# Row sums first and inverted by VectorE, one out-projection burst per head pair, DMA transposes from batch 1 on: beacon attention with a gated feed-forward block

## The chip, the cores and the metric

The kernel runs on one core of one Trainium2 chip. The metric is the device time of one execution in microseconds (us), lower is better. "Span" is the time from the first to the last instruction in a profiled execution; where the record has both for one execution, the span is 1.7 to 2.1 us shorter than the time.

Engines are named as in the profile: PE is TensorE's matmuls, PEld its weight loads, DVE is VectorE, ACT is ScalarE, POOL is GpSimd, SP is the sync engine that issues DMAs. PSUM is the memory that these kernels' matmuls write to; they share it out in banks. In lines of the profile, x8 counts instructions, and a name such as s_ps is the tile written.

## The reference, cut to what matters

```python
B, H, S, Nb, D = (8, 8, 576, 16, 64)           # attention; D_MODEL = 512, D_FF = 1536
k_all = np.concatenate([beacon_k, k], axis=2)   # 16 beacon keys + 576 keys
v_all = np.concatenate([beacon_v, v], axis=2)
scores = 0.125 * np.matmul(q, k_all.transpose(0, 1, 3, 2))
scores = np.where(causal, -1e9, scores)         # beacons are always visible
a = np.exp(scores - max); a /= a.sum(-1)        # softmax
x = np.matmul(a, v_all) -> (4608 tokens, 512)
out = (gelu(x @ w_gate) * (x @ w_val)) @ w_out  # (4608, 512) float32
```

## The kernel before: the parts that matter

Everything is computed transposed: keys, or features, on partitions and tokens along the free dimension, in bf16. For each batch there is an attention stage (four pairs of heads) and then a gate/value stage for one chunk of 512 tokens (12 tiles, 96 matmuls of 512 columns). The out-projection of the chunk before (48 matmuls, called "O" below) is spread over the attention stage as filler. There are eight batches but nine chunks; the ninth is done in the tail.

For a pair, q and k arrive token by token and must be transposed before the scores. TensorE does that through a PSUM score buffer and DVE copies it out:

```python
def transpose_pair(b, m):                     # 11 TensorE transposes, 2 DVE copies
    t_ps = psum_s.tile([P, 2, 1024], BF16, tag="s")
    for w, src in enumerate((q_ring[...], k_ring[...])):
        for j in range(4): tr(t_ps[:, w, c], src[:, j, 2*m:2*m+2, :])
        ...
    keep(nc.vector.tensor_copy(qkT[:, :, NB:SK], t_ps[:, :, 0:576]))
    keep(nc.vector.tensor_copy(qkT[:, 1, 0:NB], t_ps[:, 1, 576:592]))
```

`scores(b, m, c)` computes one of four chunks of scores, which ACT turns into exps and POOL masks. `attend` multiplies each tile of exps by V (values) and by ones (row sums, the same sum on 64 partitions), both in one PSUM tile of three banks with a single buffer. `normalize` inverts the sums on ACT as exp(-ln z) and multiplies on DVE; only then is that tile free:

```python
act(ln_sb, x_ps[:, Z0 : Z0 + S], ACT.Ln)
act(rec_sb, ln_sb, ACT.Exp, scale=-1.0)
tensor_tensor(out=xT_sb[...], in0=x_ps[:, X0 : X0 + S], in1=rec_sb, op=mult)
```

The order per pair alternates small pieces:

```python
for m in range(1, NPAIR):
    scores(b, m, 0); scores(b, m, 1)
    av(m - 1, 0, 2);  o(4);  scores(b, m, 2)
    av(m - 1, 4, 1, 3)
    if m < NPAIR - 1: transpose_pair(b, m + 1)
    o(2);  normalize(b, m - 1);  scores(b, m, 3);  o(2)
```

The softmax here doesn't subtract the row's maximum and nothing guards it: scores larger than these inputs give would overflow.

Of the kernel before, what the change touches and what calls it, by code (L numbers as in the profile page):

```python
# [8 lines left out]
P = 128  # L9
# [7 lines left out]
CH = 512  # L17
N_CHUNKS = N_TOK // CH
NPAIR = H // 2
NPERM = 2  # L20
# [16 lines left out]

# [3 lines left out]
X0 = 16  # L41
Z0 = X0 + S
# [6 lines left out]
SET_EXP = "natural_log_exp_and_others"  # L49
# [4 lines left out]
def kernel(  # L54
# [21 lines left out]
    opool = ctx.enter_context(tc.tile_pool(name="opool", bufs=2))  # L76
# [3 lines left out]

    ident = const.tile([P, P], BF16, name="ident", tag="ident")
    ones = const.tile([P, D], BF16, name="ones", tag="ones")
    nc.vector.memset(ones, 1.0)
# [3 lines left out]
    xT_sb = const.tile([P, NPAIR, N_TOK], BF16, name="xT_sb", tag="xT_sb")  # L87

    NRING = 3
    q_ring, k_ring, v_ring, qk_ring = [], [], [], []  # L90
    for r in range(NRING):
        qt = ring.tile([P, 5, H, D], BF16, name=f"q_sb{r}", tag=f"q_sb{r}")
        kt = ring.tile([P, 5, H, D], BF16, name=f"k_sb{r}", tag=f"k_sb{r}")
        vt = ring.tile([P, 5, H, D], BF16, name=f"v_sb{r}", tag=f"v_sb{r}")
        q_ring.append(qt)
        k_ring.append(kt)
        v_ring.append(vt)
    for r in range(2):
        t = ring.tile([P, 2, 640], BF16, name=f"qkT{r}", tag=f"qkT{r}")
        nc.vector.memset(t[:, 1, SK:640], 0.0)  # L100
        qk_ring.append(t)

# [5 lines left out]

    def load_qk(b):
        for src, dst in ((q, q_ring[b % NRING]), (k, k_ring[b % NRING])):  # L110
            if b < NPERM:
                dma(
                    dst[:, 0:4, :, :].rearrange("p r h d -> p (r h d)").rearrange("p (h x) -> p h x", h=H),
                    src[b, :, 0:512, :].rearrange("h (p r) d -> p h (r d)", r=4),
                )
            else:
                for j in range(4):
                    dma(dst[:, j, :, :], src[b, :, j * P : (j + 1) * P, :].rearrange("h p d -> p h d"))
            dma(dst[0:64, 4, :, :], src[b, :, 512:576, :].rearrange("h p d -> p h d"))
        dma(k_ring[b % NRING][64:80, 4, :, :], beacon_k[b].rearrange("h t d -> t h d"))  # L120

    def load_v(b):
        dst = v_ring[b % NRING]
        dma(dst[0:NB, 0, :, :], beacon_v[b].rearrange("h t d -> t h d"))
        dma(dst[NB:P, 0, :, :], v[b, :, 0:112, :].rearrange("h p d -> p h d"))
        for j in range(1, 4):
            r0 = 112 + (j - 1) * P
            dma(dst[:, j, :, :], v[b, :, r0 : r0 + P, :].rearrange("h p d -> p h d"))
        dma(dst[0:80, 4, :, :], v[b, :, 496:576, :].rearrange("h p d -> p h d"))

    def load_gate_val(i):
        fs = slice(i * 512, (i + 1) * 512)
        for w, dst in ((moe_w_gate, wg_sb), (moe_w_val, wv_sb)):
            keep(nc.gpsimd.dma_start(out=dst[:, :, fs], in_=w[:, fs].rearrange("(kk p) f -> p kk f", p=P)))

    def load_out_w():
        keep(nc.gpsimd.dma_start(out=wo_sb, in_=moe_w_out.rearrange("(ii p) m -> p ii m", p=P)))
# [6 lines left out]


    def transpose_pair(b, m):
        i = b * NPAIR + m
        t_ps = psum_s.tile([P, 2, 1024], BF16, name="t_ps", tag="s")

        def tr(out_ap, in_ap, r0=0):  # L150
            n = in_ap.shape[0]
            keep(nc.tensor.transpose(out_ap, in_ap, ident[r0 : r0 + n, r0 : r0 + n]))  # L152

        for w, src in enumerate((q_ring[b % NRING], k_ring[b % NRING])):
            by_head = src[:, 0:4, :, :].rearrange("p r h d -> p (r h d)").rearrange(
                "p (h r d) -> p h r d", h=H, r=4
            )
            for j in range(4):
                c = slice(j * P, (j + 1) * P)
                if b < NPERM:  # L160
                    for hi in range(2):
                        tr(t_ps[64 * hi : 64 * hi + 64, w, c], by_head[:, 2 * m + hi, j, :])
                else:
                    tr(t_ps[:, w, c], src[:, j, 2 * m : 2 * m + 2, :])
            tr(t_ps[:, w, 512:576], src[0:64, 4, 2 * m : 2 * m + 2, :])
        tr(t_ps[:, 1, 576:592], k_ring[b % NRING][64:80, 4, 2 * m : 2 * m + 2, :], 64)
        qkT = qk_ring[i % 2]
        if b < NPERM:
            for w in range(2):
                keep(  # L170
                    nc.vector.tensor_copy(  # L171
                        qkT[:, w, NB : NB + 512].rearrange("p (t r) -> p t r", r=4),
                        t_ps[:, w, 0:512].rearrange("p (r t) -> p t r", r=4),
                    )
                )
            keep(nc.vector.tensor_copy(qkT[:, :, NB + 512 : SK], t_ps[:, :, 512:576]))
        else:
            keep(nc.vector.tensor_copy(qkT[:, :, NB:SK], t_ps[:, :, 0:576]))  # L178
        keep(nc.vector.tensor_copy(qkT[:, 1, 0:NB], t_ps[:, 1, 576:592]))  # L179

    exp_of = {}

    def scores(b, m, c):
        i = b * NPAIR + m
        qkT = qk_ring[i % 2]
        if c == 0:
            exp_of[i] = epool.tile([P, 2, EXP_W], BF16, name="expT", tag="expT")
        expT = exp_of[i]
        s_ps = psum_s.tile([P, 2, 512], FP32, name="s_ps", tag="s")
        for t, s_lo, w, col in CHUNKS[c]:  # L190
            for hi in range(2):
                r = slice(64 * hi, 64 * hi + 64)
                mm(
                    s_ps[:, hi, col : col + w],
                    qkT[r, 1, t * P : (t + 1) * P],
                    qkT[r, 0, NB + s_lo : NB + s_lo + w],
                    True,
                    True,
                )
        o, w = CHUNK_OFF[c], CHUNK_W[c]  # L200
        act(expT[:, :, o : o + w], s_ps[:, :, 0:w], ACT.Exp, scale=QK_SCALE)
        for t, s_lo, _, _ in CHUNKS[c]:
            if s_lo != S_LO[t]:
                continue
            d = expT[0 : KROWS[t], :, EXP_OFF[t] : EXP_OFF[t] + DIAG[t]]
            keep(
                nc.gpsimd.affine_select(  # L207
                    out=d,
                    in_=d,
                    pattern=[[0, 2], [1, DIAG[t]]],  # L210
                    compare_op=ALU.is_ge,
                    fill=0.0,
                    base=NB if t == 0 else 0,
                    channel_multiplier=-1,
                )
            )

    x_of = {}

    def attend(b, m, t):  # L220
        i = b * NPAIR + m
        if t == AV_ORDER[0]:
            x_of[i] = psum_x.tile([P, 1536], FP32, name="x_ps", tag="x")
        x_ps, expT, v_sb = x_of[i], exp_of[i], v_ring[b % NRING]
        kr, first, last = KROWS[t], t == AV_ORDER[0], t == AV_ORDER[-1]
        for base, split in ((X0, 496), (Z0, 432)):
            for q0, q1 in ((S_LO[t], split), (max(split, S_LO[t]), S)):
                if q0 >= q1:
                    continue
                e0 = EXP_OFF[t] + q0 - S_LO[t]  # L230
                for hi in range(2):
                    mm(
                        x_ps[64 * hi : 64 * hi + 64, base + q0 : base + q1],
                        v_sb[0:kr, t, 2 * m + hi, :] if base == X0 else ones[0:kr, :],
                        expT[0:kr, hi, e0 : e0 + q1 - q0],
                        first and not (base == Z0 and q0 == 0),
                        last,
                        skip_group_check=True,
                    )

    def normalize(b, m):
        i = b * NPAIR + m
        x_ps = x_of.pop(i)
        del exp_of[i]
        ln_sb = npool.tile([P, S], FP32, name="ln_sb", tag="ln_sb")
        act(ln_sb, x_ps[:, Z0 : Z0 + S], ACT.Ln)
        rec_sb = npool.tile([P, S], FP32, name="rec_sb", tag="rec_sb")
        act(rec_sb, ln_sb, ACT.Exp, scale=-1.0)
        keep(
            nc.vector.tensor_tensor(  # L250
                out=xT_sb[:, m, b * S : (b + 1) * S],
                in0=x_ps[:, X0 : X0 + S],
                in1=rec_sb,
                op=ALU.mult,
            )
        )


    h_of, o_of = {}, {}

    def gate_val(ci, fi, kk_late=False):
        if fi == 0:
            h_of[ci] = hpool.tile([P, F_TILES, CH], BF16, name="hT_sb", tag="hT_sb")
# [141 lines left out]
```

## Time and profile before

| | before |
|---|---|
| time, median of 3 (lowest to highest) | 467.87 us (466.08 to 468.37) |
| span of the profiled run | 463.9 us |
| PE, DVE, ACT, POOL busy | 91%, 33%, 50%, 35% |
| one batch, from batch 3 on | 49.3 us: attention 28.3, gate/value 21.0 |
| gate/value of batch 0 begins | 45.2 us |

These are lines of the page of the kernel before: busy time of each engine, PE's busy tenths and its granted clock in 40 slices of the span, and the chain of waits that ended last, as shares of the span by engine.

```profile
PE 420.9 (91%) x3248; PEld 201.6 (43%) x3248; DVE 152.7 (33%) x259; ACT 230.9 (50%) x316; POOL 164.1 (35%) x297
...
PE   0577997999999999999999999999999999999985
...
PEclk9987999999999999999999999999999999999999
...
PE 85%; DVE 5%; ACT 4%; POOL 2%; DMA 2%; issue 1%; DVEq 0%; POOLq 0%
```

PE carries 85% of the chain and is nearly never idle after the start. That does not make the kernel as fast as PE can be: being busy includes transposes and the gaps at changes of operand shape. So I read the chain itself over one pair of batch 4 and over the end of that batch (start in us, length in us, what):

```profile
225.67 0.53 PE s_ps L140 x8
226.20 0.90 PE x_ps L140 x16
227.10 0.97 PE o_ps L140 x4
228.07 0.30 PE s_ps L140 x2
228.37 0.78 PE x_ps L140 x20
229.15 1.03 PE t_ps L152 x11
230.18 0.54 PE o_ps L140 x2
230.72 0.20 PE s_ps L140 x2
230.91 0.54 PE o_ps L140 x2
231.45 0.53 PE s_ps L140 x8
...
240.82 0.65 ACT ln_sb L143
241.50 0.69 ACT rec_sb L143
242.22 0.77 DVE xT_sb L250
243.03 0.97 PE x_ps L140 x16
```

A pair takes 231.45 - 225.67 = 5.78 us and holds 8 O. One O streaming alone takes 0.216 us (96 gate/value matmuls take 20.87 us less one switch), so 4 O should take 0.86 us; they take 0.97 here, and 2 O take 0.54 rather than 0.43. Each piece of O costs about 0.1 us extra. There are nine pieces in a pair, and I take the same for the others (an estimate from the O pieces). The transposes (t_ps) take 1.03 us. In the last lines the next values (x_ps) wait for Ln, Exp and the multiply of the pair before, because there is one bank set for them.

PE's two longest waits in the kernel before (total us, times, longest us):

```profile
PE t_ps L152 <- POOL ident masks.py:199: 12.7, 1, 12.7
PE x_ps L140 <- DVE xT_sb L250: 9.3, 8, 2.1
```

The first is the start: POOL makes the identity for the transposes only after eleven load issues, two stretches of which waited for earlier loads (0.4 and 1.8 us).

### The profile page before, as it was taken

How to read it: one execution, taken by the hardware profiler on the slowest of the kernel's cores; microseconds unless marked ns; L12 is line 12 of the kernel's file. 1: busy time of each engine (PE TensorE's matmuls, PEld its weight loads, DVE VectorE, ACT ScalarE, POOL GpSimd, SP SyncE). 2: the span in 40 equal slices, each digit the busy share in tenths (PEclk: the TensorE clock that was granted, in tenths of full speed). 3: DMA queues.
4: the chain of work that ended last, by engine and by line, in shares of the span. 5: the costliest groups of instructions: out<-in, count | busy, mean ns of one | idle time of the engine just before them, and what ended most of it. 6: DMA issues, size and time to landing. Idle time of an engine off the chain costs nothing.

```text
span 463.9 us, 7740 instructions
## 1 busy us (share of the span) xinstructions
PE 420.9 (91%) x3248; PEld 201.6 (43%) x3248; DVE 152.7 (33%) x259; ACT 230.9 (50%) x316; POOL 164.1 (35%) x297
## 2 busy tenths in 40 slices
PE   0577997999999999999999999999999999999985
PEld 0344443444454445444445445444544354444432
DVE  0222432434332432344324323343324322442321
ACT  1374445753576356644674367535763567432210
POOL 7669498283137613580339123001310032000000
PEclk9987999999999999999999999999999999999999
DMA  9999999099008901291109701000000010000111
GB/s 113 186 186 129 173 142 142 36 100 81 23 24 73 131 0 47 38 155 12 47 24 135 45 25 47 23 1 23 24 24 24 0 47 24 23 1 23 47 47 68
DMA packets 112275, 29.08 MB, mean 63 GB/s; under 512 B 98928, under 2 KB 107632, under 8 KB 112240
## 3 DMA queue, kind: packets, MB, share of 16 engines
q0 software_dynamic: 107056, 19.14, 51.9%
q1 hardware_dynamic: 5184, 9.44, 5.3%
q8 instruction: 25, 0.41, 0.3%
q14 instruction: 10, 0.08, 0.1%
HBM read 38.27 MB, written 9.44 MB: 103 GB/s over the span
## 4 chain that ended last, share of the span: by engine, by line
PE 85%; DVE 5%; ACT 4%; POOL 2%; DMA 2%; issue 1%; DVEq 0%; POOLq 0%
PE gv_ps L140 40%; PE o_ps L140 20%; PE x_ps L140 11%; PE t_ps L152 7%; PE s_ps L140 6%; DVE xT_sb L250 2%; DMA k_sb_93<-in_k_dram 2%; DVE o_sb L302 2%; ACT expT L143 2%; ACT rec_sb L143 1%; ACT ln_sb L143 1%; POOL v_sb_94 L107 1%; DVE qkT_101 L171 1%; DVE qkT_103 L171 1%; POOL q_sb_92 L107 0%
## 5 line engine op out<-in xcount | busy, mean ns | idle before, releaser
L143 ACT ACTIVATE expT<-s_ps 128x1024 bf16<-128x1024 f32 (+3 forms) x128 | 106.4, 861 | 62.0 <-PE s_ps L140 61.9
L207 POOL TENSOR_SCALAR_AFFINE_SELECT expT<-expT 128x256 bf16<-128x256 bf16 (+2 forms) x160 | 59.6, 393 | 215.9 <-ACT expT L143 215.9
L143 ACT ACTIVATE ge_sb<-gv_ps 128x512 bf16<-128x512 f32 x108 | 64.5, 597 | 123.8 <-PE gv_ps L140 123.8
L140 PE MATMUL o_ps<-wo_sb,hT_sb 128*128 128x512 bf16 x432 | 112.8, 381 | 6.9 <-DVE o_sb L302 6.9
L281 DVE TENSOR_TENSOR hT_sb<-gv_ps,ge_sb 128x512 bf16<-128x512 f32 x108 | 74.7, 692 | 117.5 <-ACT ge_sb L143 117.5
L140 PE MATMUL gv_ps<-xT_sb,wg_sb 128*128 128x512 bf16 x432 | 112.4, 380 | 0.6 <-DVE xT_sb L250 0.6
L140 PE MATMUL gv_ps<-xT_sb,wv_sb 128*128 128x512 bf16 x432 | 112.2, 379 | 0.0
L140 PEld LDWEIGHTS <-wv_sb 128*128 128x128 bf16 x432 | 42.3, 98 | 52.8 <-issue 2.9
L140 PEld LDWEIGHTS <-wg_sb 128*128 128x128 bf16 x432 | 42.2, 98 | 51.0 <-issue 0.3
L140 PEld LDWEIGHTS <-hT_sb 128*128 128x128 bf16 x432 | 34.7, 97 | 46.2 <-issue 12.0
L140 PE MATMUL x_ps<-expT,ones 128*64 128x144 bf16 (+5 forms) x576 | 49.1, 254 | 0.0
L302 DVE COPY o_sb<-o_ps 128x512 f32<-128x512 f32 x36 | 24.7, 686 | 47.0 <-PE o_ps L140 47.0
L250 DVE TENSOR_TENSOR xT_sb<-x_ps,rec_sb 128x576 bf16<-128x576 f32 x32 | 24.1, 753 | 46.2 <-ACT rec_sb L143 46.2
L143 ACT ACTIVATE ln_sb<-x_ps 128x576 f32<-128x576 f32 x32 | 20.7, 647 | 26.5 <-PE x_ps L140 26.5
L140 PEld LDWEIGHTS <-ones 128*64 128x64 bf16 (+1 forms) x576 | 23.9, 115 | 5.5 <-issue 0.7
L140 PE MATMUL s_ps<-qkT_101 64*128 64x512 bf16 (+2 forms) x192 | 22.0, 297 | 4.0 <-DVE qkT_101 L179 3.3
L140 PE MATMUL x_ps<-expT,v_sb_94 128*64 128x80 bf16 (+5 forms) x216 | 20.1, 276 | 4.2 <-DVE xT_sb L250 4.1
L140 PE MATMUL s_ps<-qkT_103 64*128 64x512 bf16 (+2 forms) x192 | 20.5, 293 | 3.4 <-DVE qkT_103 L179 3.4
L143 ACT ACTIVATE rec_sb<-ln_sb 128x576 f32<-128x576 f32 x32 | 21.9, 683 | 1.0
L140 PE MATMUL x_ps<-expT,v_sb_97 128*64 128x80 bf16 (+5 forms) x216 | 17.6, 248 | 5.0 <-DVE xT_sb L250 3.1
L178 DVE COPY qkT_103<-t_ps 128x1152 bf16<-128x1152 bf16 x12 | 9.1, 758 | 38.0 <-PE t_ps L152 38.0
L152 PE MATMUL t_ps<-ident,q_sb_92 128*64 128x128 bf16 (+2 forms) x76 | 6.9, 236 | 13.0 <-POOL ident masks.py:199 12.7
(53 smaller groups left out, 263.1 us busy)
## 6 DMA issues: line engine op xcount, KB each, us to landing
out_dram<-o_sb SPq DMA_DIRECT2D x36, 256.0 KB, 2.0
wg_sb<-in_moe_w_gate_dram POOLq DMA_DIRECT2D x3, 512.0 KB, 8.0
wv_sb<-in_moe_w_val_dram POOLq DMA_DIRECT2D x3, 512.0 KB, 9.6
wo_sb<-in_moe_w_out_dram POOLq DMA_DIRECT2D x1, 1536.0 KB, 13.0
v_sb_94<-in_v_dram POOLq DMA_DIRECT2D x9, 128.0 KB, 4.9
v_sb_97<-in_v_dram POOLq DMA_DIRECT2D x9, 128.0 KB, 4.9
q_sb_98<-in_q_dram POOLq DMA_DIRECT2D x8, 128.0 KB, 8.5
k_sb_99<-in_k_dram POOLq DMA_DIRECT2D x8, 128.0 KB, 5.6
```

Of the source, the lines that this page charges most:

```text
L107: keep(nc.gpsimd.dma_start(out=out_ap, in_=in_ap))
L140: keep(nc.tensor.matmul(out_ap, lhsT, rhs, start=start, stop=stop, **kw))
L143: keep(nc.scalar.activation(out_ap, in_ap, func, **kw))
L152: keep(nc.tensor.transpose(out_ap, in_ap, ident[r0 : r0 + n, r0 : r0 + n]))
L171: nc.vector.tensor_copy(qkT[:, w, NB : NB + 512].rearrange("p (t r) -> p t r", r=4), t_ps[:, w, 0:512].rearrange("p (r t) -> p t r", r=4),)
L178: keep(nc.vector.tensor_copy(qkT[:, :, NB:SK], t_ps[:, :, 0:576]))
L207: nc.gpsimd.affine_select(out=d, in_=d, pattern=[[0, 2], [1, DIAG[t]]], compare_op=ALU.is_ge, fill=0.0, base=NB if t == 0 else 0, channel_ ...
L250: nc.vector.tensor_tensor(out=xT_sb[:, m, b * S : (b + 1) * S], in0=x_ps[:, X0 : X0 + S], in1=rec_sb, op=ALU.mult,)
L281: nc.vector.tensor_tensor(out=h_of[ci][:, fi, :], in0=gv_ps[:, 1, :], in1=ge_sb, op=ALU.mult)
L302: keep(nc.vector.tensor_copy(o_sb[:, ti, :], o_ps))
```

## The change

Its intent: take the transposes of q and k off PE and DVE from batch 1 on; give the row sums their own PSUM banks and compute them before the values, so that they can be inverted while the values run; invert on DVE, so that ACT only does exps and gelus; run fewer, longer bursts on PE; and start sooner.

```diff
@@ inversion: 32x32 block transposes bring equal sums onto one column, so the reciprocal is 18 wide
+    def invert(b, m):
+        zt = npool.tile([P, S], FP32)
+        nc.vector.transpose(zt, z_of[i][:, Z0 : Z0 + S])
+        nc.vector.reciprocal(rz, zt.rearrange("p (n j) -> p n j", j=32)[:, :, 0])
+        nc.vector.transpose(rec..., rz.unsqueeze(2).to_broadcast([P, NBLK, 32]))
-        act(ln_sb, x_ps[:, Z0 : Z0 + S], ACT.Ln)
-        act(rec_sb, ln_sb, ACT.Exp, scale=-1.0)
@@ sums in two banks of their own (z_ps), with 64 columns of the values; the other values in x_ps
+    def sums(b, m):
+        z_ps = psum_x.tile([P, 1024], FP32, tag="z"); ...
+    def values(b, m):
+        x_ps = psum_x.tile([P, X_SPLIT], FP32, tag="x"); ...
-            x_of[i] = psum_x.tile([P, 1536], FP32, name="x_ps", tag="x")
@@ DMA transposes from batch 1 on: ten of up to 128x512 on the SP queue
+    def xbar_transpose(b):
+        for j in range(5):
+            nc.sync.dma_start_transpose(out=qkT[:, 1, :, j*P : j*P+n], in_=kt[0:n, j, :])
+            nc.sync.dma_start_transpose(out=qkT[:, 0, :, c : c+n], in_=qt[0:n, j, :])
@@ start: V of batch 0 as float32 on SP, warm-up matmuls, q and k two heads at a time, early identity
+    load_v_fp32(0); heat(10); load_runs(0, 2); load_beacon(dma, bk0, beacon_k[0])
@@ order: S = score chunks, Z = sums, V = values, O = out-projection matmuls
+        if b == 1:   attention(b, "S0 L S1 S23", ..., "S0 S1 Z S2 V S3 O12", "Z V")
+        elif b == 2: attention(b, "S01 O12 S23 O12", "S01 Z V O12 S23 O12", ..., "S01 Z V S23 O12", "Z V")
+        else:        attention(b, "O4 S01 O8 S23 O2", "S01 Z V S23 O10", "S01 Z V S23 O12", "S01 Z V S23 O8", "Z V")
+        load_qk(b + 1); load_v(b + 1)
+        gate_val_first(b, 0 if b == 1 else 4 if b>2 else 0)   # two tiles begun without the last pair
+        xbar_transpose(b + 1)
+        gate_val(b, 2, F_TILES)
```

(Cut: the loads, the transposes of batch 0, the tail, which keeps its order.) In batch 1 only 12 O run and batch 2 makes up for it with 84, because the out-projection's weights are now loaded in batch 1.

## The prediction

> **What bounds it.** TensorE: busy 421 of the 463.9 us span, 85% of the chain of waits (page, parts 1 and 4); ACT 50%, DVE 33%, POOL 35%. In the timeline a batch from the third on repeats every 49.3 us: a gate/value stage of 96 matmuls back to back (20.87 us, 216 ns each) and an attention stage of 28.4 us. At that rate of columns (my estimate) attention needs only 10.4 us of out-projection, 2.8 of scores, 5.6 of values and sums. The other 10 us:
> - TensorE transposes: 11 per pair, 1.03 us in the chain, 4.1 us per batch; 7.1% of the span.
> - Switches between operand shapes: six out-projection matmuls between score bursts take 1.40 us, not 1.29: about 0.1 us a switch, nine per pair. [...]
> - Waits: for the single output bank (0.5 us), for normalisation to free the value bank (1.0 us near each batch's end), for the transposes' copies.
>
> At the start the first matmul comes at 12.7 us, gate/value of batch 0 at 45.2 us.
>
> **What the change does.**
> 1. From batch 1, DMA transposes replace TensorE's: minus 4.1 us of TensorE and 3.7 us of DVE copies per batch. Added: ten 128x512 transposes per batch on the SP queue, hidden behind the 21 us gate/value stage if they finish. Their loads need about 10 us of issue (0.88 us each) and 4–8 us to land. [...]
> 2. Bursts: four per pair (two scores, sums+values, two scores, out-projection): half the switches, minus 1.8 us per batch.
> 3. The inversion moves from ACT (0.65+0.68 us) to DVE (two 576-column transposes of about 0.75, a small reciprocal, multiplies of 0.2+0.7: about 2.6 us, estimated from the 576-column multiply's 0.75). It starts before the values and hides under out-projection. ACT's 42.6 us fall away off the critical path.
> 4. New waits per batch: exp table load and ACT-bound first slot 1 us; fourth score chunk waiting for exp 0.2 us per pair; two gate/value tiles finishing together 1.2 us.
> 5. Start: smaller first loads, warm-up matmuls, V by another queue. First scores at 10 us instead of 15.9, gate/value(0) at about 32 us[...].
> 6. Batch 1 has only 12 out-projections and is ACT-bound (13.8 us of exp): 18.5 us of attention. Batch 2 takes 84: 30 us.
>
> **Sum (span).** To the end of gate/value(0) 54; batch 1 40.5; batch 2 52; batches 3–7 five times 44.4 = 222; tail 49.6 as before (one output bank). Total 418, plus 4 us between span and time: **421 us**, range 403 to 441. Chances: faster 0.95, same 0.03, slower 0.02.
>
> **What would show it.** TensorE transposes only in batch 0; a period of 43–45.5 us from batch 3; gate/value about 21–22 us plus 0.9 us of out-projection; no TensorE wait on DMA at batch starts; gate/value(0) at 30–34 us; ACT busy about 190 us, DVE near 190.
>
> **What would make it wrong.** DMA transposes over 2.5 us each, or behind late loads: every batch starts 5 to 15 us late, which could eat the gain. DVE transposes twice as slow would stall the last pair before gate/value. DMA saturation could delay batch 1.

(Three passages are cut from it, as no run of this case shows them: a rule about switches, beside the measured 0.1 us; a figure for a DMA transpose, with the estimate of its issue time that rested on it; and a claim about what limits the start of gate/value. No term of the sum is among them: the terms give 418, and 418 + 4 = 422; the text on record says 421.)

## The result, and the profile after

The changed kernel took 427.42 us (median of 3, 427.19 to 427.60) against 467.87: faster, with a ratio of 0.9157 (95% interval 0.912 to 0.9193). Ratios here are not quite the ratio of the medians quoted. The span is 425.5 us. Each later experiment has its own runs of the kernel before beside it (medians 466.0 to 467.4 us), so differences between experiments are taken from the ratios, times 467 us.

Where the span went, with the stages bounded by the first score matmul of each batch in PE's timeline:

| stretch | before | after | difference |
|---|---|---|---|
| start to the scores of batch 1 | 67.0 | 59.4 | -7.6 |
| batches 1 and 2 | 101.9 | 96.0 | -5.9 |
| batches 3 to 6 | 197.3 (49.3 each) | 177.4 (44.35 each) | -19.9 |
| batch 7 and the tail | 97.7 | 92.7 | -5.0 |
| span | 463.9 | 425.5 | -38.4 |

The same lines of the page as before, for the changed kernel:

```profile
PE 387.8 (91%) x2814; PEld 180.0 (42%) x2814; DVE 190.8 (45%) x324; ACT 188.6 (44%) x255; POOL 169.4 (40%) x302
...
PE   5778958898999999999999999999999999999985
...
PEclk9589988999999999999999999999999999999999
...
PE 71%; DMA 11%; SPq 7%; DVE 6%; ACT 3%; issue 2%; POOL 1%; DVEq 0%; ACTq 0%; POOLq 0%
```

PE lost 33 us of busy time. 42 us left ACT and 38 us came to DVE. The share of busy time of PE is the same 91% in both kernels, which is why it says little. DMA and SPq now have 18% of the chain.

The chain in batch 5, from the landing of a DMA transpose to the start of gate/value:

```profile
238.52 6.24 DMA qkT<-k_sb
244.77 0.60 PE s_ps L200 x8
...
253.58 0.53 PE s_ps L200 x8
254.11 0.99 PE z_ps L200 x22
255.10 0.60 PE x_ps L200 x10
255.70 0.51 PE s_ps L200 x4
256.21 2.70 PE o_ps L200 x12
258.90 0.53 PE s_ps L200 x8
...
264.95 2.70 PE gv_ps L200 x12
267.65 0.86 PE o_ps L200 x4
...
268.98 0.61 ACT ge_sb L203
269.61 0.70 DVE hT_sb L364
270.36 17.44 PE gv_ps L200 x80
```

A pair takes 258.90 - 253.58 = 5.32 us and holds 12 O, not 8: it does 0.86 us more work in 0.46 us less. The four pieces of the pair follow each other without a wait. The first two lines show a new wait: this batch began when a DMA transpose landed, after 0.7 us of waiting on PE. The last lines show another: two gate/value tiles end together, and PE waits for the gelu and the product of the first.

PE's waits in the changed kernel:

```profile
PE gv_ps L200 <- DVE hT_sb L364: 7.8, 8, 1.0
...
PE s_ps L200 <- DMA qkT<-q_sb: 3.5, 2, 3.0
```

The inversion on DVE (groups; busy us, mean ns of one, then the idle time before them):

```profile
L315 DVE STREAM_TRANSPOSE zt<-z_ps 128x576 f32<-128x576 f32 x32 | 25.0, 782 | 40.6 <-PE z_ps L200 40.6
...
L320 DVE STREAM_TRANSPOSE rec<-rz 128x576 f32<-128x576 f32 x32 | 24.9, 778 | 1.1
...
L317 DVE RECIPROCAL rz<-zt 128x18 f32<-128x18 f32 x32 | 8.6, 267 | 1.1
```

With the multiplies (223 and 680 ns) that is 2.73 us per pair; the prediction said 2.6.

SP's timeline shows the first and the last of the ten DMA transposes for batch 1, and PE's timeline the scores that wait for them (start, length, operation, idle before it and what ended that):

```profile
40.19 1.29 SPq L162 DMA_TRANSPOSE qkT<-k_sb  x1
...
54.55 1.20 SPq L165 DMA_TRANSPOSE qkT<-q_sb  x1
```

```profile
59.36 0.60 PE L200 MATMUL s_ps<-qkT 64*128 64x512 bf16 x8 [3.02 <-DMA qkT<-q_sb]
...
62.62 1.01 PE L200 MATMUL s_ps<-qkT 64*128 64x512 bf16 x8 [0.48 <-ACT expT L203]
```

Most issues take 1.2 to 1.3 us on SP (the longest 2.9; no run shows why), and the data land 7.6 us after them in the median. So ten of them need 19 us from the first issue to the last landing, about as long as the gate/value stage. In batch 1 PE waited 3.0 us for them. The same eight score matmuls then took 0.60 us at first and 1.01 us a little later: the granted clock is 0.83 over that attention stage. The wait is not shown to be the cause of that: in a_early_loads below PE did not wait for a transpose at this place, and the same second burst took 1.01 us as well, at a granted clock of 0.84 over the stage.

### The profile page after: what moved, and what is told of

The parts are those of the page before. It is cut to its first block, busy times and chain, and to the rows that moved or that the text cites. A ratio compares the mean times of both kernels' runs of the same rounds, so it can differ in the third digit from the quotient of the medians.

```text
span 425.5 us, 7034 instructions
## 1 busy us (share of the span) xinstructions
PE 387.8 (91%) x2814; PEld 180.0 (42%) x2814; DVE 190.8 (45%) x324; ACT 188.6 (44%) x255; POOL 169.4 (40%) x302
## 4 chain that ended last, share of the span: by engine, by line
PE 71%; DMA 11%; SPq 7%; DVE 6%; ACT 3%; issue 2%; POOL 1%; DVEq 0%; ACTq 0%; POOLq 0%
PE gv_ps L200 33%; PE o_ps L200 22%; PE z_ps L200 7%; PE s_ps L200 6%; SPq L162 4%; PE x_ps L200 4%; DMA wo_sb<-in_moe_w_out_dram 3%; SPq L165 3%; DMA qkT<-q_sb 3%; DVE o_sb L402 2%; DVE hT_sb L364 2%; ACT ge_sb L203 2%; DMA bk<-in_beacon_k_dram 2%; DMA k_sb<-in_k_dram 2%; DMA qkT<-k_sb 1%
## 5 line engine op out<-in xcount | busy, mean ns | idle before, releaser
L200 PEld LDWEIGHTS <-wg_sb 128*128 128x128 bf16 x432 | 41.6, 98 | 60.0 <-issue 11.8
L200 PE MATMUL s_ps<-qkT 64*128 64x80 bf16 (+5 forms) x384 | 41.3, 296 | 12.6 <-DMA qkT<-q_sb 3.5
L315 DVE STREAM_TRANSPOSE zt<-z_ps 128x576 f32<-128x576 f32 x32 | 25.0, 782 | 40.6 <-PE z_ps L200 40.6
L200 PE MATMUL z_ps<-expT,ones 128*64 128x464 bf16 (+5 forms) x384 | 36.2, 300 | 1.1 <-DVE xT_sb L332 1.1
L112 POOL DMA_DIRECT2D v_sb<-in_v_dram x35 | 29.7, 869 | 10.9 <-DMA k_sb<-in_k_dram 5.7
L200 PEld LDWEIGHTS <-qkT 64*128 64x128 bf16 x384 | 14.7, 95 | 42.9 <-issue 28.9
L112 POOL DMA_DIRECT2D k_sb<-in_k_dram x35 | 30.2, 864 | 1.0 <-DMA wv_sb<-in_moe_w_val_dram 1.0
L112 POOL DMA_DIRECT2D q_sb<-in_q_dram x35 | 30.6, 874 | 0.0
L200 PEld LDWEIGHTS <-v_sb 128*64 128x64 bf16 (+1 forms) x640 | 22.0, 114 | 8.4 <-issue 2.6
L320 DVE STREAM_TRANSPOSE rec<-rz 128x576 f32<-128x576 f32 x32 | 24.9, 778 | 1.1
L200 PE MATMUL x_ps<-expT,v_sb 128*64 128x512 bf16 (+4 forms) x320 | 25.4, 285 | 0.0
```

The lines of the kernel that those rows point to most:

```text
L112: keep(nc.gpsimd.dma_start(out=out_ap, in_=in_ap))
L200: keep(nc.tensor.matmul(out_ap, lhsT, rhs, start=start, stop=stop, **kw))
L315: keep(nc.vector.transpose(zt, z_of[i][:, Z0 : Z0 + S]))
L320: nc.vector.transpose(rec.rearrange("p (n j) -> p n j", j=32), rz.unsqueeze(2).to_broadcast([P, NBLK, 32]))
```

## The experiments

Twelve kernels ran. Names with a_ start from the changed kernel, names with b_ from the kernel before. All gave correct results.

| run | what | time, us | ratio to before | 95% interval |
|---|---|---|---|---|
| (the change) | | 427.42 | 0.9157 | 0.912 to 0.9193 |
| a_pe_transpose | transposes back on PE | 458.36 | 0.9816 | 0.9781 to 0.9851 |
| a_act_invert | inversion back on ACT | 427.54 | 0.9173 | 0.9133 to 0.9212 |
| a_fragments | bursts broken up | 434.30 | 0.9309 | 0.9276 to 0.9343 |
| b_dma_transpose | only the DMA transposes | 446.15 | 0.9561 | 0.9535 to 0.9588 |
| b_dma_dve | and the DVE inversion | 462.94 | 0.9920 | 0.9895 to 0.9945 |
| a_burst_last | 12 O behind the last values | 421.30 | 0.9031 | 0.9004 to 0.9059 |
| a_early_loads | loads inside attention | 426.90 | 0.9163 | 0.9112 to 0.9213 |
| a_noheat | no warm-up matmuls | 426.15 | 0.9131 | 0.9105 to 0.9157 |
| a_v_pool | V of batch 0 by POOL | 424.60 | 0.9091 | 0.9065 to 0.9116 |
| a_act_batch0 | ACT inverts in batch 0 | 425.39 | 0.9110 | 0.9079 to 0.9141 |
| a_combined | five edits together | 420.43 | 0.9012 | 0.8983 to 0.9042 |
| a_combined2 | five edits, one exchanged | 415.00 | 0.8893 | 0.8862 to 0.8923 |

The theory at the start was that of the prediction: the gain is PE time, above all the transposes, then the switches; the inversion and ACT's relief are off the critical path, or nearly. The rival was that the new order is what gains and the transposes would have fitted into waits.

### a_pe_transpose: the transposes back on PE

```diff
+    def pe_transpose(b, m):   # ten TensorE transposes into a score buffer, two DVE copies
+        ...
-        xbar_transpose(b + 1)
-        gate_val(b, 2, F_TILES)
+        gate_val(b, 2, F_TILES - 1)
+        pe_transpose(b + 1, 0)
+        gate_val(b, F_TILES - 1, F_TILES)
-  "S01 Z V S23 O10", "S01 Z V S23 O12", ...
+  "S01 Z V S23 O4 T2 O6", "S01 Z V S23 O4 T3 O8", ...
```

> The changed kernel with TensorE transposes again from batch 1 on (11 per pair into a score buffer, two copies by VectorE), everything else kept. Theory 1 (TensorE time is what the DMA transposes bought): 28 pairs x about 1.05 us of transposes and 0.2 us of two switches give back 35 us, less about 6 us of waits for DMA transposes that vanish: 450 to 462 us. Rival (the new order of the bursts is what gained, transposes would fit in waits): under 440 us.

Measured: 458.36 us, (0.9816 - 0.9157) x 467 = 30.8 us slower than the change. This is inside what the theory expected, and far from the rival. Without the DMA transposes, all the rest of the change together gains only (1 - 0.9816) x 467 = 8.6 us, and in the traces 8.7 us lie before the scores of batch 1 (58.3 us instead of 67.0); after them the rest of the change gains nothing net.

The 30.8 us are not all transposes. PE's busy time rose by 20.9 us (from 387.8 to 408.7); ten transposes take 0.75 to 0.90 us per pair in the chain here. The rest is waits and switches that come with them, for example (before gate/value the wait was 7.8 us in the change):

```profile
PE gv_ps L200 <- DVE hT_sb L376: 12.6, 15, 1.0
PE s_ps L200 <- DVE qkT L224: 5.3, 8, 1.5
```

### b_dma_transpose: the DMA transposes alone

```diff
-NPERM = 2
+NPERM = 1
+            if fi == 1 and b + 1 < B:
+                xbar_transpose(b + 1)
-            if m < NPAIR - 1:
+            if m < NPAIR - 1 and b < NPERM:
                 transpose_pair(b, m + 1)
```

> The kernel before with only the DMA transposes from batch 1 on (q and k rings of two, loads a batch earlier than in the changed kernel; its bursts, start and ScalarE inversion kept). If the parts add up independently, 28 pairs x 1.03 us of TensorE vanish: 437 to 440 us. Theory 1 (the parts need each other: at about 4.7 us of TensorE per pair ScalarE's 4.77 us is the limit, and the value bank still waits for the inversion): gain of only 15 to 23 us, 445 to 453 us.

Measured: 446.15 us, a gain of 20.5 us and not 29: the parts do need each other. The chain says how. This is one pair of batch 4 in that kernel, from exp chunk 2 to the next scores:

```profile
218.38 0.94 ACT expT L158
219.32 0.55 ACT ln_sb L158
...
219.90 0.68 ACT rec_sb L158
220.58 0.41 ACT expT L158
...
221.04 0.38 PE s_ps L155 x6
```

ACT ran these in program order. Ln and Exp of the pair before stand between the exps of two score chunks, and the scores of the next pair wait for the second of these to free a score buffer. PE waits only 0.33 us at this place, but the pair is now held at 5.33 us by ACT. In PE's timeline the pair from 215.57 to 220.32 us fell from 5.78 to 4.75 us; the next, to 225.65, fell only to 5.33. The end of the batch, from the last pair's first score to gate/value, shrank by 0.67 us and not by 1.03 (9.54 to 8.87): there the values still wait 1.0 us for their single bank.

### b_dma_dve: and the inversion on DVE, still in the old order

```diff
-        act(ln_sb, x_ps[:, Z0 : Z0 + S], ACT.Ln)
-        act(rec_sb, ln_sb, ACT.Exp, scale=-1.0)
+        nc.vector.transpose(zt, x_ps[:, Z0 : Z0 + S])
+        nc.vector.reciprocal(rz, ...)
+        nc.vector.transpose(rec_sb, rz broadcast)
```

> The kernel before with the DMA transposes and with the inversion on VectorE (two transposes and a reciprocal) in place of Ln and Exp; its fine-grained order and its one shared value bank kept. Theory (with DMA transposes alone, Ln and Exp stood between the exps of two score chunks and held the scores back 0.33 us and more per pair): the wait of the scores for exp goes, 2 to 6 us less than the 446.2 us of DMA transposes alone: 440 to 444 us. Rival (what limits that kernel is the switches and the value bank; the VectorE chain is longer, about 2.6 against 2.1 us, so the bank waits more): 446 to 450 us.

Measured: 462.94 us, 16.8 us slower than with the DMA transposes alone. The theory fell, and the rival had the direction but not the size. The chain of one pair:

```profile
228.01 0.79 DVE zt L270
...
228.83 0.28 DVE rz L272
...
229.13 0.79 DVE rec_sb L275
...
229.94 0.77 DVE xT_sb L280
...
230.75 0.97 PE x_ps L155 x16
```

The wait for exp is gone, as the theory said. But sums and values share one PSUM tile and end together, and the next pair's values wait for the end of transposing, inverting, transposing and multiplying, 2.7 us in all, at three pairs of every batch and not only at its end; PE itself stood still for 1.0 to 1.6 us of each in this batch. PE waited 31.3 us for xT_sb in this kernel (24 times, up to 2.7 us), against 7.3 us with Ln and Exp. The DVE inversion is harmless only in the new order with "sums first, in banks of their own", where its start is earlier and PE hardly waits for it (1.1 us for xT_sb, once). Which of the two, the order or the banks, does it was not tested apart.

### a_act_invert: the inversion back on ACT, in the new order

```diff
-SET_EXP = "exp_and_others"
+SET_EXP = "natural_log_exp_and_others"
-        nc.vector.transpose(...); nc.vector.reciprocal(...); nc.vector.transpose(...)
+        act(ln, z_of[i][:, Z0 : Z0 + S], ACT.Ln)
+        act(rec, ln, ACT.Exp, scale=-1.0)
```

> The changed kernel with the row sums inverted by ScalarE again (Ln, then Exp of minus it, 0.65+0.68 us per pair) in place of the two VectorE transposes and the reciprocal. Theory 1 (ScalarE then has 3.44+1.33 = 4.77 us of work per pair against slots of 4.0 to 5.3 us, so it becomes a limit): 0.5 to 1.5 us more per batch, 431 to 440 us. Rival A (inversion is off the critical path wherever it runs): 427 us within 1.5. Rival B (it is where most of the gain is): over 445 us.

Measured: 427.54 us; the ratio differs by 0.0016 from the change, well inside both intervals. Theory 1 fell and rival A holds for the total: in the new order it comes out the same whichever engine inverts. ACT became busier (226.3 us instead of 188.6) and DVE less busy (132.7 instead of 190.8), both off the critical path. The trace shows two small effects that cancel: the attention stage of most batches is 0.4 us longer, and batch 0 is shorter (its gate/value starts at 31.2 us and not 34.3). The second is tried below.

### a_fragments: the bursts broken up

```diff
-  "O4 S01 O8 S23 O2", "S01 Z V S23 O10", "S01 Z V S23 O12", "S01 Z V S23 O8", "Z V"
+  "O4 S0 O4 S1 O4 S2 O1 S3 O1", "S0 S1 Z O4 S2 V O3 S3 O3", "S0 S1 Z O4 S2 V O4 S3 O4", "S0 S1 Z O3 S2 V O3 S3 O2", "Z V"
```

(and likewise in batch 2)

> The changed kernel with the bursts of batches 2 to 7 broken up: single score chunks with pieces of 1 to 8 out-projection matmuls between them, sums and values apart; the same matmuls. Theory 1 (a switch of operand shape costs about 0.1 us): 4 to 5 more switches per pair, 24 pairs: 9 to 12 us more, 433 to 440 us. Rival (the pieces also fill waits for exp, so order does not matter): 427 us within 2.

Measured: 434.30 us, 7.1 us slower. In a batch from the third on there are 16 more changes of operand shape (34 instead of 18), and the period grew from 44.35 to 45.50 us on average, the attention stage by 1.36: 0.07 to 0.085 us each. A little of it is another wait: PE's for the output bank rose from 6.2 to 7.9 us over the span. What PE does in these gaps the traces do not show. The bursts gain real time, but a quarter of what the transposes gain.

### a_burst_last: O behind the last values

```diff
-  "S01 Z V S23 O12", "S01 Z V S23 O8", "Z V"
+  "S01 Z V S23 O8", "S01 Z V S23 O4", "Z V O12"
-        gate_val_first(b, 0 if b == 1 else 4 if b>2 else 0)
+        gate_val(b, 0, 2)
```

(and likewise in batches 1 and 2)

> The changed kernel with 12 of each batch's out-projection matmuls moved behind the last sums and values, to cover the inversion of the last pair there, and without the split start of gate/value. Theory (the 7.8 us that gate/value waits for hT_sb, 1.0 us at each start, comes from two tiles ending together in the split start): 5 to 8 us less, 419 to 423 us. Rival (the wait is only moved: gate/value then waits for the last multiply, or the shortened slots for exp): 426 to 429 us.

Measured: 421.30 us, 5.9 us faster than the change, as expected. PE's wait for hT_sb before gate/value fell from 7.8 us (8 times) to 1.0 us (once, in batch 0, which has no O). 12 O take 2.6 us and cover the inversion of the last pair just as well as the split start did. A part of the wait came back elsewhere: the sums (z_ps) wait 3.5 us for xT_sb, not 1.1.

### a_early_loads: q and k earlier

```diff
+  "O4 S01 O8 S23 O2 Q0", "S01 Z V S23 O10 Q1", "S01 Z V S23 O12 Q2", "S01 Z V S23 O8 Q3"   # Q = a piece of the loads
-        load_qk(b + 1)          # after attention
```

> The changed kernel with the q and k loads of the next batch issued in four pieces inside the attention stage (for batch 1 before the last third of the weights), so that the DMA transposes can start earlier. Theory (the DMA transposes end late because their loads start only at the end of attention[...]): 3 to 7 us less, 420 to 425 us. Rival (the transposes are bound by their own rate, or the issues on GpSimd now delay the masks): 427 us or more.

(Cut from it: the clause that said what the late landing costs, because part of it was a claim about the clock that no run shows. PE's waits for the transposes in the changed kernel were 3.0 us at batch 1, 0.5 at batch 3 and 0.7 at batch 5.)

Measured: 426.90 us, no difference. The waits for DMA transposes did vanish from PE's longest waits, and batch 1 began at 56.8 us and not 59.4. But its attention stage grew from 19.6 to 21.5 us. Of that, 1.5 us lie in its first pair: ACT first had to finish the last gelu and load its table for exp (1.28 us), so the first exp began at 58.76 us, only 1.1 us earlier than in the change (59.85), where both had run during the wait for the transposes. At the end of the stage the first ten matmuls of the last sums took 1.39 us, not 0.87, while masks ran late behind load issues on POOL (about 0.9 us each). The wait was moved, not removed. In batch 0, where loads now also stand in front of masks, PE's waits have a new line:

```profile
PE z_ps L201 <- POOL expT L272: 1.2, 1, 1.2
```

### a_noheat: no warm-up matmuls

```diff
-    heat(10)
```

> The changed kernel without the ten warm-up matmuls. Theory (the clock falls back in the 3 to 4 us of waiting for the first loads after them, as the granted clock of the second fortieth, 0.5, suggests, so they buy nothing): 427.4 within 1.5 us. Rival (they shorten batch 0's attention): 429 to 433 us.

Measured: 426.15 us, 1.2 us faster by the ratios, with overlapping intervals. So the warm-up buys nothing here. The first eight score matmuls took 1.03 us with it (at 10.98 us) and without it (at 10.07 us), against 0.60 for the first eight of batch 5. The granted clock of the second fortieth of the span is 0.5 in the changed kernel although the warm-up matmuls ran until 5.7 us. What they gave was gone by the first scores: in the changed kernel twelve transposes took 0.45 us at 6.45 us, just after the warm-up, and twelve of the same shape 0.69 us at 9.86 us, after a wait of 2.85 us (granted clock 0.90 from 5.7 to 9.8 us, 0.50 from there to 11); without the warm-up both took 0.69 us. Whether leaving them out gains is not settled.

### a_v_pool: V of batch 0 through POOL

```diff
-    load_v_fp32(0)                       # SP queue, float32, DVE casts (taken out too)
+    load_v(0)                            # POOL queue, after load_runs(2, 4)
```

> The changed kernel with the V of batch 0 loaded and cast through the GpSimd queue behind the first two head loads, as the kernel before does, in place of the SP queue and a VectorE cast. Theory (GpSimd is idle between about 5 and 12.7 us and V is needed only at about 16 us, so the separate queue for V is not what moved the start): 427.4 within 2 us. Rival (V on its own queue is what lets batch 0 start early): 430 to 436 us.

Measured: 424.60 us, 3.1 us faster than the change; neither theory said that. In the changed kernel V is in flight on SP's queue while the first q, the first k and the 16 KB of beacon keys are wanted, and the beacon keys took 6.9 us to land; with V behind them they took 3.3 us. The first scores came at 7.1 us instead of 11.0 (9.3 to 11.0 in the traces of all variants that keep V on SP, 7.7 in the last one below, which does not). With V (as float32) on SP the core's DMA engines moved more in the first fortieth of the span (159 against 93 GB/s), but what was needed first came later.

The earlier scores are not the gain itself. Gate/value of batch 0 began at 33.75 us instead of 34.31; its attention ran at a granted clock of 0.55 (0.75 in the change), and the first ten matmuls of the sums took 1.55, 1.55, 1.55 and 1.41 us in its four pairs (1.54, 1.55, 0.88 and 0.88). But the loads of batch 1 were issued 0.7 us earlier and landed sooner, its DMA transposes began at 37.39 us instead of 40.19, PE's wait for them fell from 3.0 to 0.3 us, and batch 1 began at 55.84 us instead of 59.36.

### a_act_batch0: ACT inverts in batch 0 only

```diff
+        if b == 0:
+            act(ln, z_of[i][:, Z0 : Z0 + S], ACT.Ln)
+            act(rec, ln, ACT.Exp, scale=-1.0)
+            rec_of[i] = rec
+            return
```

(and the table set with Ln loaded at the start)

> The changed kernel with the inversion by Ln and Exp on ScalarE in batch 0 only. Theory (in batch 0 VectorE does the transposes' copies, the casts and the inversions in turn, and the chain of waits runs through them, so there the inversion does sit on the critical path; with ScalarE inverting everywhere gate/value started at 31.2 us, not 34.3): 424 to 426 us. Rival (that start was chance, from the first loads): 427 to 428 us.

Measured: 425.39 us, 2.2 us faster by the ratios, with intervals that just overlap. Gate/value of batch 0 began at 31.4 us instead of 34.3, but batch 1 only at 57.2 instead of 59.4, for PE then waited 4.0 us for its DMA transposes. The earlier start is not chance: in the other traces with the change's order of batch 0 and DVE inverting (a_burst_last, a_fragments, a_pe_transpose, a_noheat) it lies between 33.5 and 34.95 us, and with ACT inverting in a_act_invert at 31.2. In batch 0 DVE copies transposes, casts V and inverts, one after the other, and the chain of waits runs through it. There the engine that inverts does matter, a little.

### a_combined and a_combined2: versions meant to beat both

The first joins a_burst_last, a_early_loads (for batch 1 only at its end), a_noheat, a_act_batch0 and a tail that uses two output banks in turn and keeps 8 O for its last wait. The second leaves the early loads out and takes a_v_pool in.

```diff
+                if tail[0] and ti % 2:
+                    o_ps_of[0] = psum_x.tile([P, D_MODEL], FP32, tag="x")   # the free value bank
-        o(4)
-    o(OUT_UNITS)
+        o(4 if fi < 10 else 0)
+    o(OUT_UNITS + 8)
```

> A version meant to beat both: the burst behind the last values, loads of the next batch in pieces inside attention (for batch 1 only at its end), no warm-up matmuls, ScalarE inversion in batch 0, two output banks in turn in the tail and 8 out-projection matmuls kept for its last wait. If the gains add: 421.3 (burst alone), minus about 1 (warm-up), minus 2 to 3 (batch 0), minus 3 to 4 (tail: four waits of 0.74 us and one of 1.15), minus about 2 (batch starts): 410 to 415 us. If the transposes or the loads take the gain back: 416 to 421 us.

Measured: 420.43 us, only 0.9 us better than a_burst_last by the ratios, with overlapping intervals. The tail gave its 4.2 us (from the gate/value of batch 7 to the last matmul 62.3 us instead of 66.5), but the attention stages of batches 3 to 6 were 0.8 us longer than in a_burst_last and that of batch 1 2.2 us, with masks late behind load issues in the former.

> The combined version without the early loads, which had cost more in late masks than they gave, and with V of batch 0 behind the first head loads on the GpSimd queue: burst behind the last values, ScalarE inversion in batch 0, no warm-up, two output banks in the tail. If the gains add to the 421.3 us of the burst alone: tail minus 4.2 (66.5 to 62.3 us as in the first combined version), start minus 2 to 4: 413 to 416 us. If the start gains only move the wait to the DMA transposes of batch 1: 416 to 418 us.

Measured: 415.00 us (median of 7), ratio 0.8893: 2.9% faster than the change, the best version here. The gains added up within 416 us. Its profile was taken in its slowest run, 418.56 us, and shows what is left at the start: gate/value of batch 0 begins at 29.2 us, but PE then waits for the DMA transposes of batch 1:

```profile
PE s_ps L200 <- DMA qkT<-k_sb: 5.6, 1, 5.6
```

## Why the prediction was right

The forecast was 421 us in a range of 403 to 441; 427.42 was measured, a gain of 40 us where 47 was forecast. Point by point:

- **What bounds it.** Right. In the 49.3 us period the gate/value matmuls kept their pace, 0.216 us each before and after, and attention gave the time.
- **Step 1, DMA transposes.** Right in mechanism: 28 pairs at 1.03 us are 29 us; taking the step back cost 30.8 us, and adding it alone gained 20.5. That 29 and 30.8 are so close is partly luck, as PE's busy time accounts for 20.9 of the 30.8. Most issues took 1.2 to 1.3 us; the author's estimate of that is cut from the text above, as it rested on no run. The statement "no TensorE wait on DMA at batch starts" was wrong: landing takes 7.6 us after the issue, which I had not put in the sum, and PE waited 3.0 us for them in batch 1, 0.5 in batch 3 and 0.7 in batch 5.
- **Step 2, bursts.** Right in direction. 1.8 us per batch was forecast; breaking them up again cost 1.15 us per batch from the third on, 7.1 us in all.
- **Step 3, inversion on DVE.** "ACT's 42.6 us fall away off the critical path" was right: a_act_invert took the same time. The size was right too (2.73 us against 2.6). What the prediction did not see is that this step would have cost 16.8 us in the old order; the new order with its separate banks makes it harmless.
- **Step 4, new waits.** The two gate/value tiles ending together were right: 1.0 us per batch against 1.2, and a_burst_last confirmed the cause by removing it. The waits for exp were over-estimated: 2.7 us in the whole span (PE's waits), not 1 us plus 0.8 us per batch. With step 2 mis-sized the other way the period came out right, 44.35 us against 44.4; that so exact a match came from errors that cancel is luck.
- **Step 5, the start.** Forecast 10 us for the first scores, 32 for gate/value of batch 0 and 54 for its end; measured 11.0, 34.3, and 59.4 for the next scores. Of that miss of 5.4 us, 3.0 are the wait for the DMA transposes and the rest is batch 0: DVE as a limit there (2.9 us in a_act_batch0), while V's queue delayed the first scores but gate/value of batch 0 by only 0.6 us.
- **Step 6, batches 1 and 2.** Forecast 40.5 and 52 us; measured 41.6 and 54.5.

The span was forecast at 418 and came to 425.5. The miss of 7.5 us is 5.4 at the start, 1.1 in batch 1, 2.5 in batch 2, and -1.5 in the rest. The smaller terms of the sum were off; the period of the later batches was not. In the time, about 2 us of that miss were made up by chance: 4 us were added between span and time, and 1.7 were measured in the profiled run.

What stays open: whether the warm-up matmuls cost anything, whether the order or the separate banks make the DVE inversion harmless, what the smaller first loads and the early identity gained at the start (they were not undone), why the granted clock is low in batch 1, and how much of the 5.6 us wait at batch 1 in the best version could be had without delaying masks.

## What to carry to other kernels

Cost a change by what it takes from the engine that carries the chain, per repetition, and check what it hands to the other engines: here the transposes were most of the gain, and 40 us of work moved between two engines off the chain were worth nothing. A part that is harmless in one order can cost most of the gain in another (16.8 of 20.5 us here), because there a buffer waited for the end of a longer chain (PE waited 31.3 us for xT_sb in b_dma_dve, 1.1 in the changed kernel); so undo parts in both kernels before calling one the cause. When work moves to a DMA queue, add the time from issue to landing (7.6 us in the median here), not only the issue (mostly 1.2 to 1.3 us), and see what the loads and the masks on the issuing engine delay.

## What these runs measured of the new instructions

- Ten DMA transposes of up to 128x512 bf16 (592 + 576 rows of 1 KB, 1.2 MB) took 19.2 us from the first issue (40.19) to the scores that waited for the last landing (59.36): about 62 GB/s, with other loads in flight. A plain load of q of 128 KB landed 6.0 us after its issue in the median, a transpose 7.6. One instruction of 128 KB per 1.22 us of issue (the median of q's) would be about 107 GB/s (an estimate). What these instructions on one queue would reach without other loads was not run.
- A DMA transpose of 128x512 mostly held SP 1.2 to 1.3 us, but its data landed 7.6 us after the issue in the median (4.8 to 9.4).
- A block transpose on VectorE in float32 at 128x576 took 782 ns from PSUM and 778 ns from a broadcast SBUF operand; an 18-wide reciprocal took 267 ns.
- A change of operand shape on PE cost about 0.1 us: 0.11 us read from the chain (4 O between scores and values took 0.97 us, not 0.86), 0.07 to 0.085 us from 16 added changes per batch.
